# Sparse attention and two gated layers on one core: the outside keys of both heads of the first and last block are transposed together, and the sums of exponentials are finished on GpSimd

## The chip, the core and the metric

The kernel runs on one core of one Trainium2 chip. The metric is the time on the device in microseconds (us) of one execution. Five engines run side by side, each through its own instructions in order: TensorE (PE in the views, its weight loads PEld), VectorE (DVE), ScalarE (ACT), GpSimd (POOL) and the queue that issues transfers (SP).

## What is computed

Attention with a window of 32 keys to each side plus 32 global keys, for 4 batches, 8 heads, 512 local tokens and a head size of 64; its output goes through two gated layers.

```python
s_g = scale * q_g @ k_all.T                     # 32 global queries see all 544 keys
out_g = softmax(s_g) @ v_all
mask = np.abs(pos[:, None] - pos[None, :]) <= 32
s_l = np.concatenate([scale * q_l @ k_g.T, np.where(mask, scale * q_l @ k_l.T, -1e9)], -1)
out_l = softmax(s_l) @ np.concatenate([v_g, v_l])    # softmax: exp(s - max) / (sum + 1e-9)
x = heads_side_by_side(np.concatenate([out_g, out_l]))        # 2176 x 512
x = (sigmoid(x @ w_gate) * (x @ w_val)) @ w_out               # d_ff 1536
h = x @ w_in                                                  # d_ff 2048
out = (P(h) / Q(h)) @ w_out2                                  # P cubic, Q quadratic in |h|
```

## The kernel before

The kernel has three stages: attention (to about 114.6 us of the span), the first gated layer, and the rational layer. The change touches attention alone.

**Units and blocks.** Attention works on 16 units u0 to u15: a unit is one batch and one pair of heads (j = 0 and 1). A unit has four blocks c of 128 queries. An inner block (c = 1, 2) sees WIN = 224 keys: its 128 own keys, 32 global keys, and 32 keys on either side of it. An outer block (c = 0, 3) has a neighbour on one side only and sees 192 keys: 128 own and 64 outside. "Half 0" of a unit is blocks 0 and 1, "half 1" blocks 2 and 3.

**The steps of a unit**, each a small function:

- `load` (L232) issues the transfers: `kn` (keys), `qn` (queries), `vn` (values of own keys), `wn` (values of outside keys).
- `s_mm` (L256): scores of a half on TensorE into a `pair` of PSUM banks (L265). `s_max` (L270): on VectorE, scores plus mask into `p`, with the row's maximum (L277). `s_exp` (L281): on ScalarE, exponentials in place, their sum to `sum[:, n, 0]` (L285); `sum[:, n, 1]` holds 1e-9.
- `s_add` (L289) adds the two columns of `sum` into `r` (L291), `s_rec` (L293) takes the reciprocal (L295), both on VectorE; `s_norm` (L297) multiplies `p` of one block by it on GpSimd (L301).
- `t_mm` (L364): four 128x128 transposes of a block on TensorE into one PSUM bank: own keys of both heads (L368), then outside keys of both heads (L370), each padded to 128 with the last own keys. `t_out` (L374) copies the bank into `to` (L376), on ScalarE for c = 1, 3 and on VectorE for c = 0, 2.
- `v_own`, `v_edge` (L386, L395): the products with `vn` and `wn`. `wn` has zeros in its first 32 rows, and the part of `p` behind an outer block's 192 keys is zero.
- Of the global queries, per pair of units: `g_mm` (L310), `g_max`, `g_exp`, `g_rec`, `g_norm` (GpSimd, L336), `g_turn` (L342, L343), `e_own` (VectorE, L354), `e_edge` (ScalarE, L360).
- `x_hi`, `x_lo`, `x_g`, `x_out` write the result into `xh`, `xl` for the next stage (L414, L419, L427, L434, L225, L438).

**What sets the order.** The table `STEPS` gives each step a place for the first two units, a pattern of two units that repeats for the middle ones, and the last two units. All steps are sorted by place and issued in that order; each engine runs its share strictly in it. PSUM has two `pair` tiles and four `bank` tiles, handed out in the same order. The table also interleaves the preparation of the first gated weights (`w_mag`, `w_bits`, `w_add`, `w_hi`, `w_lo`).

## Time and profile before

| | |
|---|---|
| Median of 3 runs | 898.29 us (898.19 to 898.74) |
| The profiled execution: its own time | 898.83 us |
| Span in its profile | 896.9 us |
| Granted clock of TensorE | 1.00 of full speed in all 40 slices |
| Busy, share of span: PE / PEld / DVE / ACT / POOL | 99% / 82% / 84% / 64% / 64% |
| Chain of work that ended last | 87% PE, 7% DVE, 1% ACT, 1% POOL |
| Attention, first two-unit pattern to end | about 12.7 us for two units, end at 114.6 us |

Shares over the span mix stages: in attention DVE and ACT are far busier than the average says, and POOL waits for others. The stage has to be read by stretches, and then by single instructions in order of time.

### The profile page before, as it was taken

What the parts mean: (1) busy time and instruction counts of PE and PEld (TensorE: products, weight loads), DVE (VectorE), ACT (ScalarE), POOL (GpSimd) and SP (SyncE); (2) the same over time, 40 slices, a digit from 0 to 9 for tenths busy, and PEclk for the clock granted to TensorE, in tenths of its full rate; (3) what the DMA queues carried; (4) which work ended last, traced back from release to release, by engine and by line L of the source; (5) the groups of instructions that cost most, each with busy time, mean ns of one, the idle gap of its engine ahead of it and who ended that gap; (6) DMA issues with size and microseconds to landing.
All of it is one profiled execution on the core that took longest, in us unless ns stands there. A gap on an engine that the chain in (4) does not pass through costs nothing.

```text
span 896.9 us, 13592 instructions
## 1 busy us (share of the span) xinstructions
PE 889.3 (99%) x4592; PEld 737.3 (82%) x4592; DVE 750.1 (84%) x1300; ACT 576.2 (64%) x1161; POOL 576.0 (64%) x470
## 2 busy tenths in 40 slices
PE   8999999999999999999999999999999999999997
PEld 6788988888888888888888888888888888888886
DVE  6999967988889888766868699987788899888886
ACT  6999865445554344354444488777777787777773
POOL 5768765767767485476767767544555676666564
PEclk9999999999999999999999999999999999999999
DMA  9775274767667686999998960022001300110112
GB/s 307 242 219 170 83 280 169 267 227 252 232 236 262 231 300 217 322 339 321 341 352 331 360 213 1 1 94 94 1 1 51 114 24 1 43 51 1 48 59 94
DMA packets 60372, 155.87 MB, mean 174 GB/s; under 512 B 7056, under 2 KB 8720, under 8 KB 60304
## 3 DMA queue, kind: packets, MB, share of 16 engines
q1 hardware_dynamic: 60208, 154.89, 49.7%
q8 instruction: 36, 0.59, 0.3%
q14 instruction: 32, 0.26, 0.1%
q10 hardware_dynamic: 96, 0.13, 0.1%
HBM read 102.83 MB, written 52.17 MB: 173 GB/s over the span
## 4 chain that ended last, share of the span: by engine, by line
PE 87%; DVE 7%; ACT 1%; POOL 1%; issue 0%; POOLq 0%; ACTq 0%
PE rp L1255 6%; PE rp L1257 6%; PE rp L1256 6%; PE rp L725 5%; PE rp L723 5%; PE rp L724 5%; PE p L844 4%; PE p L842 4%; PE p L843 4%; PE pg L723 3%; PE pg L724 3%; PE pg L725 3%; PE pv L723 3%; PE pv L724 3%; PE pv L725 3%; PE pair L265 2%
## 5 line engine op out<-in xcount | busy, mean ns | idle before, releaser
L1172 POOL TENSOR_TENSOR v<-v,u 128x512 f32<-128x512 f32 x68 | 93.4, 1374 | 105.6 <-ACT v L1168 103.4
L1226 POOL TENSOR_TENSOR rgl<-t,rgh 128x512 fp32r<-128x512 f32 x64 | 89.1, 1393 | 40.6 <-POOL v L1172 17.3
L1255 PE MATMUL rp<-wide,rgh 128*128 128x512 f32 x204 | 79.5, 390 | 0.6 <-DVE racc L1276 0.6
L1257 PE MATMUL rp<-wide,rgl 128*128 128x512 f32 x204 | 79.4, 389 | 0.0
L1256 PE MATMUL rp<-wide,rgh 128*128 128x512 f32 x204 | 79.4, 389 | 0.0
L1165 ACT ACTIVATE u<-rp 128x512 f32<-128x512 f32 x68 | 40.5, 596 | 60.2 <-PE rp L725 57.3
L1180 DVE TENSOR_TENSOR t<-rp,t 128x512 f32<-128x512 f32 x68 | 46.7, 687 | 38.7 <-ACT t L1176 37.6
L723 PE MATMUL rp<-yh,wide 128*128 128x512 f32 x192 | 75.0, 391 | 0.0
L1205 DVE SCALAR_TENSOR_TENSOR t<-t,co,v 128x512 f32<-128x512 f32 x68 | 72.9, 1072 | 2.4
L770 ACT CAST gh<-t 128x512 fp32r<-128x512 f32 x38 | 23.6, 620 | 79.7 <-DVE t L763 76.0
L725 PE MATMUL rp<-yh,wide 128*128 128x512 f32 x192 | 74.7, 389 | 0.0
L724 PE MATMUL rp<-yl,wide 128*128 128x512 f32 x192 | 74.7, 389 | 0.0
L1201 DVE SCALAR_TENSOR_TENSOR v<-v,u 128x512 f32<-128x512 f32 x68 | 73.8, 1085 | 0.0
L301 POOL TENSOR_TENSOR p<-p,r 128x384 f32<-128x384 f32 (+1 forms) x64 | 55.4, 889 | 28.4 <-DVE r L295 13.9
L1197 DVE SCALAR_TENSOR_TENSOR v<-v,u 128x512 f32<-128x512 f32 x68 | 61.7, 908 | 1.1 <-ACT u L1193 1.1
L285 ACT ACTIVATE p<-p,mx 128x224 f32<-128x224 f32 (+1 forms) x128 | 58.5, 467 | 6.1 <-DVE mx L277 6.1
L856 DVE TENSOR_TENSOR gacc<-p,gacc 128x512 f32<-128x512 f32 x80 | 51.2, 680 | 10.1 <-PE p L844 10.1
L1168 ACT ACTIVATE v<-u,co 128x512 f32<-128x512 f32 x68 | 55.6, 817 | 2.3
L775 DVE TENSOR_TENSOR gl<-t,gh 128x512 fp32r<-128x512 f32 x38 | 37.4, 985 | 23.1 <-ACT gh L770 23.0
L1189 ACT ACTIVATE u<-v,co 128x512 f32<-128x512 f32 x68 | 49.2, 724 | 6.2 <-POOL v L1172 6.0
L1176 ACT ACTIVATE t<-rp,co 128x512 f32<-128x512 f32 x68 | 51.7, 761 | 0.0
L1214 ACT CAST rgh<-t 128x512 fp32r<-128x512 f32 x64 | 39.1, 611 | 18.0 <-DVE t L1205 18.0
(724 smaller groups left out, 2913.1 us busy)
## 6 DMA issues: line engine op xcount, KB each, us to landing
raw1gv<-in_w_gate_val SPq DMA_DIRECT2D x24, 512.0 KB, 4.2
raw2in<-in_w_in SPq DMA_DIRECT2D x16, 512.0 KB, 5.0
raw2out<-in_w_out SPq DMA_DIRECT2D x16, 512.0 KB, 5.0
kn<-in_k_l SPq DMA_DIRECT2D x15, 448.0 KB, 5.5
raw1out<-in_w_out SPq DMA_DIRECT2D x12, 512.0 KB, 4.2
vn<-in_v_l SPq DMA_DIRECT2D x16, 256.0 KB, 3.2
out<-racc SPq DMA_DIRECT2D x16, 256.0 KB, 2.0
qn<-in_q_l SPq DMA_DIRECT2D x15, 256.0 KB, 4.5
```

The costliest lines, as they stand in the source:

```text
L285: nc.scalar.activation(p, p, AF.Exp, bias=s["mx", half][:, n : n + 1], scale=-1.0, accum_out=s["sm", half][:, n, 0:1])
L723: nc.tensor.matmul(ps, wh, mh[:, k], start=k == 0, stop=False)
L724: nc.tensor.matmul(ps, wh, ml[:, k], start=False, stop=False)
L725: nc.tensor.matmul(ps, wl, mh[:, k], start=False, stop=k == 3)
L1172: nc.gpsimd.tensor_tensor(s["v"], s["v"], s["u"], ALU.mult)
L1197: nc.vector.scalar_tensor_tensor(s["v"], s["v"], Q_CONST, s["u"], ALU.add, ALU.mult)
L1201: nc.vector.scalar_tensor_tensor(s["v"], s["v"], 2.0, s["u"], ALU.subtract, ALU.mult)
L1205: nc.vector.scalar_tensor_tensor(s["t1"], s["t1"], a0, s["v"], ALU.add, ALU.mult)
L1226: nc.gpsimd.tensor_tensor(s["gl"], s["t1"], s["gh"].bitcast(F32), ALU.subtract)
L1255: nc.tensor.matmul(ps, gh[:, w], wh, start=k == 0, stop=False)
L1256: nc.tensor.matmul(ps, gh[:, w], wl, start=False, stop=False)
L1257: nc.tensor.matmul(ps, gl[:, w], wh, start=False, stop=k == G - 1)
```

## The change

The table `STEPS` is left as it is. What changes:

- **Keys on both sides.** For an outer block the 64 outside keys lie in `kn` both ahead of and behind the 128 own keys. Head 0 uses own keys then outside keys, head 1 outside keys then own keys; the two results of 192 are put side by side in `p`, so that the middle 128 of the 384 columns are the outside keys of both heads.
- **One transpose for both heads.** `t_mm` of an outer block issues three transposes, not four. `t_out` copies three of them. `v_edge` multiplies that one part by `wn`, now laid out on the host as full 128 rows with zeros in the place of the other head. The memsets of `wn` and of the end of `p` go.
- **Masks.** Masks of up to 320 columns are put together by five copies on VectorE; before it was two copies.
- **Global queries.** `g_mm` reads its 512 own keys as two pieces of 256 (six matmuls, not four). `g_norm` gets one more GpSimd copy of 128x32. `e_edge` becomes two VectorE copies of 64x32 per unit in place of one ScalarE copy of 128x64.
- **Sums.** `s_add` moves from VectorE (a reduction) to GpSimd (an addition of two columns).
- **Transfers.** `kn` grows from 448 to 480 KB a unit, `wn` from 192 to 256 KB.

```diff
-    kept = dict(kn=slots(one, "kn", 4, [128, NBLK, WIN]), ...
+    kept = dict(kn=slots(one, "kn", 4, [128, KAT[-1]]), ...
...
-    for t in wn:
-        nc.gpsimd.memset(t[0 : 128 - EDGE], 0.0)
...
-    for t in kept["p"].tiles:
-        for c in (0, NBLK - 1):
-            nc.gpsimd.memset(t[:, c, :, KEYS[c] :], 0.0)
...
     def s_add(u, half):
         r = st[u]["r", half] = two.tile([128, 4], F32, tag="r", name=f"r{u}_{half}", bufs=6)
-        nc.vector.tensor_reduce(r, st[u]["sm", half], mybir.AxisListType.X, ALU.add)
+        n = st[u]["sm", half]
+        nc.gpsimd.tensor_tensor(r, n[:, :, 0], n[:, :, 1], ALU.add)
...
-        for at, n, keys in ((0, S, lambda k: k[:, :, 0:128]), (S, SG, lambda k: k[:, 0, 128:160])):
+        for at, n, keys in ((0, 256, lambda k: own(k, 64, 0, KAT[1] - 64)), (256, 256, lambda k: own(k, 384, 96, 64 + WIN)),
+                            (S, SG, lambda k: k[:, 384 : 384 + SG])):
...
         nc.gpsimd.tensor_tensor(n, n, st[u]["gsm"].to_broadcast([128, S + SG]), ALU.mult)
+        copy(pgn[u // 2 % 2][:, S + 64 : S + 64 + SG], n[:, S:])
...
-        at = 64 * (u % 2)
-        src = st[u - u % 2]["ge"][:, at : at + 64].rearrange("p (h g) -> p h g", h=2)
-        nc.scalar.copy(turned(u)[:, 0, 2:4, 128:160], src)
+        for j in range(2):
+            rows, at = slice(64 * j, 64 * j + 64), 64 * (u % 2) + SG * j
+            nc.vector.tensor_copy(turned(u)[rows, 0, 2, 128:160], st[u - u % 2]["ge"][rows, at : at + SG])
...
-            nc.tensor.transpose(ps[:, 128 * j : 128 * j + 128], s["p"][:, c, j, 0:128], ident)
-        for j in range(2):
-            nc.tensor.transpose(ps[:, 256 + 128 * j : 384 + 128 * j], s["p"][:, c, j, EDGE:WIN], ident)
+            own = probs(u, c, j)[:, KEYS[c] - 128 :] if c in OUTER and j else probs(u, c, j)[:, 0:128]
+            nc.tensor.transpose(ps[:, 128 * j : 128 * j + 128], own, ident)
+        if c in OUTER:
+            nc.tensor.transpose(ps[:, 256:384], s["p"][:, c].rearrange("p j k -> p (j k)")[:, 128:256], ident)
+        else:
+            for j in range(2):
+                nc.tensor.transpose(ps[:, 256 + 128 * j : 384 + 128 * j], s["p"][:, c, j, EDGE:WIN], ident)
...
-        (nc.scalar.copy if c in T_ACT else nc.vector.tensor_copy)(turned(u)[:, c, :, at : at + 128], src)
+        (nc.scalar.copy if c in T_ACT else nc.vector.tensor_copy)(turned(u)[:, c, 0:n, at : at + 128], src)
...
-                             turned(u)[:, c, 2 + j, SG * (c % 2) : SG * (c % 2) + n],
+                             turned(u)[:, c, 2 + (0 if c in OUTER else j), SG * (c % 2) : SG * (c % 2) + n],
```

**Where `s_add` lands in the queues, at the start.** GpSimd's order for unit u0. `p_111` is u0's `p`, `pgn_125` the global queries' `p`; `r_1_...` belongs to half 1 and `r_0_...` to half 0. Before:

```order
L301 TENSOR_TENSOR p_111<-p_111,r_1_227 128x448 [waits DVE_49,Activation_49]
L336 TENSOR_TENSOR pgn_125<-pgn_125,gsm_218 128x544 [waits DVE_49,Activation_49]
L301 TENSOR_TENSOR p_111<-p_111,r_0_260 128x2x192 [waits DVE_49]
L301 TENSOR_TENSOR p_111<-p_111,r_0_260 128x448 [waits Activation_49]
L301 TENSOR_TENSOR p_111<-p_111,r_1_227 128x2x192
```

Now:

```order
L314 TENSOR_TENSOR p_111<-p_111,r_1_223 128x448 [waits DVE_49]
L351 TENSOR_TENSOR pgn_125<-pgn_125,gsm_214 128x544 [waits DVE_49,Activation_49]
L231 TENSOR_TENSOR pgn_125<-pgn_125,zero 128x32 [waits Pool_49]
L301 TENSOR_TENSOR r_0_257<-sum_132 128x4 [waits Activation_49]
L314 TENSOR_TENSOR p_111<-p_111,r_0_257 128x384 [waits DVE_49]
L314 TENSOR_TENSOR p_111<-p_111,r_0_257 128x448
L314 TENSOR_TENSOR p_111<-p_111,r_1_223 128x384
```

The sum of half 0 now stands behind the global queries' normalization and its new copy on GpSimd.

**The same at the end.** GpSimd's order for the last units. `p_112` is u13's, `p_113` u14's, `p_111` u15's; L434, L225 and L438 are `x_out`. Before:

```order
L301 TENSOR_TENSOR p_112<-p_112,r_1_1464 128x2x192 [waits DVE_49,PE_49,Activation_49]
L301 TENSOR_TENSOR p_112<-p_112,r_1_1464 128x448
L301 TENSOR_TENSOR p_113<-p_113,r_0_1502 128x2x192 [waits DVE_49,PE_49,Activation_49]
L301 TENSOR_TENSOR p_113<-p_113,r_0_1502 128x448
L336 TENSOR_TENSOR pgn_126<-pgn_126,gsm_1403 128x544 [waits DVE_49]
L301 TENSOR_TENSOR p_113<-p_113,r_1_1493 128x2x192 [waits Activation_49]
L301 TENSOR_TENSOR p_113<-p_113,r_1_1493 128x448 [waits PE_49]
L434 TENSOR_TENSOR xga_169<-xga_169 128x4x32 [waits DVE_49]
```

Now (twelve rows, in which the sums of u14's half 1 and half 0 and of u15's half 0 and half 1 stand between the normalizations):

```order
L301 TENSOR_TENSOR r_1_1498<-sum_137 128x4 [waits Activation_49]
L314 TENSOR_TENSOR p_112<-p_112,r_1_1469 128x384 [waits DVE_49,PE_49]
L314 TENSOR_TENSOR p_112<-p_112,r_1_1469 128x448
L301 TENSOR_TENSOR r_0_1507<-sum_136 128x4
L314 TENSOR_TENSOR p_113<-p_113,r_0_1507 128x384 [waits DVE_49,PE_49]
L314 TENSOR_TENSOR p_113<-p_113,r_0_1507 128x448
L351 TENSOR_TENSOR pgn_126<-pgn_126,gsm_1408 128x544 [waits DVE_49]
L231 TENSOR_TENSOR pgn_126<-pgn_126,zero 128x32 [waits Pool_49]
L301 TENSOR_TENSOR r_0_1580<-sum_132 128x4 [waits Activation_49]
L314 TENSOR_TENSOR p_113<-p_113,r_1_1498 128x384
L301 TENSOR_TENSOR r_1_1603<-sum_133 128x4 [waits Activation_49]
L314 TENSOR_TENSOR p_113<-p_113,r_1_1498 128x448 [waits PE_49]
```

Two normalizations of u13 now come after a sum that needs u14's exponentials, and u14's last one after a sum that needs u15's.

VectorE's order at the same place, before:

```order
L291 TENSOR_REDUCE r_1_1493<-sum_140 128x4 [waits Activation_49]
L295 RECIPROCAL r_1_1493<-r_1_1493 128x4 [waits DVE_49]
L291 TENSOR_REDUCE r_0_1502<-sum_139 128x4
L295 RECIPROCAL r_0_1502<-r_0_1502 128x4 [waits DVE_49]
L427 COPY xga_169<-bank_96 128x32 [waits PE_49]
L331 TENSOR_SCALAR gsm_1403<-gsm_1403 128x1
```

Now:

```order
L305 RECIPROCAL r_1_1498<-r_1_1498 128x4 [waits Pool_49]
L305 RECIPROCAL r_0_1507<-r_0_1507 128x4 [waits Pool_49]
L448 COPY xga_163<-bank_96 128x32 [waits PE_49,Activation_49]
L346 TENSOR_SCALAR gsm_1408<-gsm_1408 128x1
L347 RECIPROCAL gsm_1408<-gsm_1408 128x1 [waits DVE_49]
```

The two reductions are gone, and both reciprocals wait for GpSimd.

## Rows read from the trace of the kernel before

**Rows 1.** Busy time by stretch: us, PE, PEld, DVE, ACT, POOL, clock, DMA share, GB/s.

```profile
25.00:30.00 5.00, 5.00 (x45) 3.29 (x43) 4.93 (x34) 5.00 (x23) 2.65 (x3) 1.00 0.99 314
50.00:100.00 50.00, 50.00 (x560) 44.28 (x556) 46.60 (x237) 46.88 (x177) 35.62 (x43) 1.00 0.58 177
250.00:300.00 50.00, 50.00 (x224) 41.34 (x223) 44.58 (x58) 25.28 (x48) 32.13 (x24) 1.00 0.68 235
```

**Rows 2.** TensorE in order of time: start us, us, engine, line, tiles [idle before].

```profile
76.41 1.11 PE L310 MATMUL pair<-kn,qgn 128*64 128x512 f32 x8
77.46 0.44 PE L368 MATMUL bank<-ident,p 128*128 128x128 f32 x2
...
79.91 1.68 PE L265 MATMUL pair<-kn,qn 64*128 64x192 f32 x16
...
92.59 1.68 PE L265 MATMUL pair<-kn,qn 64*128 64x192 f32 x16
...
94.69 0.38 PE L368 MATMUL bank<-ident,p 128*128 128x128 f32 x2
...
95.13 0.38 PE L368 MATMUL bank<-ident,p 128*128 128x128 f32 x2
...
110.40 0.49 PE L386 MATMUL bank<-to,vn 128*64 128x160 f32 x4
```

**Rows 3.** Idle time inside the two-unit pattern: VectorE and GpSimd in order of time.

```profile
88.52 0.19 DVE L427 COPY xga<-bank 128x32 f32<-128x32 f32 x1 [1.14 <-ACT xh L414]
...
81.96 1.72 POOL L301 TENSOR_TENSOR p<-p,r 128x384 f32<-128x384 f32 x2 [1.86 <-DVE r L295]
```

**Rows 4.** Groups by line and shape, 0 to 135 us: count | busy us, mean ns.

```profile
L301 POOL TENSOR_TENSOR p<-p,r 128x448 f32<-128x448 f32 x32 | 30.5, 952 | 10.7 <-DVE r L295 10.5 <-DVE xga L427 0.2
L301 POOL TENSOR_TENSOR p<-p,r 128x384 f32<-128x384 f32 x32 | 26.5, 827 | 17.7 <-ACT p L285 12.1 <-DVE r L295 3.4 <-PE pair L265 0.8
...
L376 DVE COPY to<-bank 128x512 f32<-128x512 f32 x32 | 21.0, 678 | 0.6 <-PE bank L370 0.6
...
L427 DVE COPY xga<-bank 128x32 f32<-128x32 f32 x32 | 5.6, 182 | 6.0 <-ACT xh L414 5.5 <-PE bank L395 0.4
...
L360 ACT COPY to<-bank 128x64 f32<-128x64 f32 x16 | 2.5, 217 | 0.0
...
L208 POOL MEMSET sum<- 128x8 f32 x6 | 0.3, 94 | 0.0
```

**Rows 5.** The start: GpSimd and VectorE in order of time.

```profile
12.47 1.09 POOL L336 TENSOR_TENSOR pgn<-pgn,gsm 128x544 f32<-128x544 f32 x1
14.03 2.50 POOL L301 TENSOR_TENSOR p<-p,r 128x384 f32<-128x384 f32 x3 [0.46 <-DVE r L295]
...
13.58 0.16 DVE L291 TENSOR_REDUCE r<-sum 128x4 f32<-128x8 f32 x1
13.77 0.18 DVE L295 RECIPROCAL r<-r 128x4 f32<-128x4 f32 x1
```

**Rows 6.** The end: ScalarE, VectorE and GpSimd in order of time.

```profile
99.03 0.20 ACT L285 ACTIVATION_READ_ACCUMULATOR p<-p,mx 128x1 f32 x1
...
105.51 0.19 ACT L285 ACTIVATION_READ_ACCUMULATOR p<-p,mx 128x1 f32 x1
...
99.72 0.18 DVE L295 RECIPROCAL r<-r 128x4 f32<-128x4 f32 x1
...
100.57 0.19 DVE L427 COPY xga<-bank 128x32 f32<-128x32 f32 x1 [0.33 <-ACT xh L414]
...
103.38 0.08 DVE L277 DVE_READ_ACCUMULATOR2_ANT mx<- 128x1 f32 x1
...
104.48 0.46 POOL L434 TENSOR_TENSOR xga<-xga 128x128 f32<-128x128 f32 x1
...
106.12 1.72 POOL L301 TENSOR_TENSOR p<-p,r 128x448 f32<-128x448 f32 x2 [0.18 <-DVE xga L427]
108.00 1.72 POOL L301 TENSOR_TENSOR p<-p,r 128x384 f32<-128x384 f32 x2 [0.16 <-DVE r L295]
```

More of the change, by code (lines that the diff above doesn't have):

```diff
@@ L189, in attention, with mask_of, probs @@
     st = [dict() for _ in units]
-    masks = one.tile([128, 2, WIN], F32, name="masks")
-    m = masks[:, 1]
-    mask_of = [masks[:, 0]] + [m] * (NBLK - 1)
+    masks = one.tile([128, 3, 320], F32, name="masks")
+    m = masks[:, 1, 0:WIN]
+    def mask_of(c, j):
+        if c in OUTER:
+            return masks[:, 2 if c else 0, 128 * j : 128 * j + KEYS[c]]
+        return m
+    def probs(u, c, j):
+        if c in OUTER:
+            return st[u]["p"][:, c].rearrange("p j k -> p (j k)")[:, j * KEYS[c] : (j + 1) * KEYS[c]]
+        return st[u]["p"][:, c, j]
     still = one.tile([128, 128], F32, name="still")
@@ L199, in attention @@
     nc.vector.memset(m, 0.0)
-    pgn = [one.tile([128, S + EDGE], F32, name=f"pgn{i}") for i in range(2)]
+    pgn = [one.tile([128, S + 128], F32, name=f"pgn{i}") for i in range(2)]
     wn = [one.tile([128, NBLK, 128], F32, name=f"wn{i}") for i in range(3)]
@@ L264, in s_mm @@
                 rows = slice(64 * j, 64 * j + 64)
-                nc.tensor.matmul(ps[:, j, i * WIN : i * WIN + KEYS[c]], s["qn"][rows, c], s["kn"][rows, c, 0 : KEYS[c]],
+                at, to = KAT[c] + (64 if c in OUTER and j == 0 else 0), i * WIN
+                nc.tensor.matmul(ps[:, j, to : to + KEYS[c]], s["qn"][rows, c], s["kn"][rows, at : at + KEYS[c]],
                                  start=True, stop=True)
@@ L297, in s_norm @@
     def s_norm(u, half, i):
-        n = KEYS[2 * half + i]
-        p = st[u]["p"][:, 2 * half + i, :, 0:n]
+        c = 2 * half + i
+        n = KEYS[c]
+        p = st[u]["p"][:, c]
+        if c in OUTER:
+            p = p.rearrange("p j k -> p (j k)")[:, 0 : 2 * n].rearrange("p (j k) -> p j k", j=2)
         r = st[u]["r", half][:, 2 * i : 2 * i + 2].unsqueeze(2).to_broadcast([128, 2, n])
@@ L1369, in laid @@
     own, edge = pairs(x["k_l"], x.pop("k_g"))
-    x["k_l"] = np.concatenate([own, edge], axis=1).transpose(2, 3, 4, 0, 1)
+    out = [edge[c, 0:64] for c in OUTER]
+    k = [out[0], own[0], out[0], own[1], edge[1], own[2], edge[2], out[1], own[3], out[1]]
+    x["k_l"] = np.concatenate(k).transpose(1, 2, 3, 0)
     own, edge = pairs(x["v_l"], x.pop("v_g"))
-    x["v_l"], x["w_l"] = own.transpose(2, 3, 1, 0, 4), edge.transpose(2, 3, 1, 0, 4)
+    w = np.zeros((NBLK, 128) + edge.shape[2:], edge.dtype)
+    for c in range(NBLK):
+        if c in OUTER:
+            for j in range(2):
+                w[c, 64 * j : 64 * j + 64, ..., 64 * j : 64 * j + 64] = edge[c, 0:64, ..., 64 * j : 64 * j + 64]
+        else:
+            w[c, 128 - EDGE :] = edge[c]
+    x["v_l"], x["w_l"] = own.transpose(2, 3, 1, 0, 4), w.transpose(2, 3, 1, 0, 4)
     q = x["q_g"].reshape(B, 2, 2, 2, SG, D)
```

23 lines of the change are left out of this document (15 added, 8 removed).

## The prediction

> **What bounds the kernel now.** I read the busy time by stretch first. TensorE is busy for all 50 us of 50 to 100 and of 250 to 300 [rows 1]: both in attention and in the gated layers the end is set by TensorE, at full clock. So a microsecond by which attention's matmuls end earlier or later is, to a first reading, a microsecond of the kernel: behind attention nothing is changed. But inside attention the reader should see how little room there is: from 50 to 100 us VectorE is busy 46.6 and ScalarE 46.9 of 50, and from 25 to 30 us, while the units start up, ScalarE is busy without a gap and VectorE 4.93 of 5 [rows 1]. There it is these two that set the pace.
>
> Second, TensorE in order of time. The same row of scores returns at 79.91 and 92.59 [rows 2]: two units take 12.68 us. In that pattern the other engines have some room: VectorE stands still for 1.14 us before 88.52, GpSimd for 1.86 us before 81.96 [rows 3]. Third, the end of attention, engine by engine [rows 6]: there the pattern breaks off, GpSimd works through its last normalizations until 109.7 (108.00 + 1.72), and TensorE's last transposes end at 110.40 [rows 2], just behind it.
>
> **What is removed from TensorE.** Two transposes in each unit, 32 in all. From 94.69 to 95.13 four transposes are issued [rows 2], 0.11 us each: 3.5 us. It counts only where TensorE sets the pace. That is not so for u0 to u2 (before about 33 us), nor, as shown below, for the end (u11 to u15). Between lie u3 to u10: 16 transposes, **-1.8 us**.
>
> **What is added to TensorE.** `g_mm` issues 12 records where it issued 8; the columns are the same. The eight take 1.05 us (76.41 to 77.46 [rows 2]). If the loads of weights stay hidden behind 256 columns, this costs nothing; I take that, since 0.11 us transposes hide a load of 128 columns each. If each extra record costs as much as an eighth of the row, it is 32 x 0.13 = 4 us; I hold a quarter of that for an upper bound, 1 us.
>
> **ScalarE and VectorE in the pattern.** ScalarE loses `e_edge` (0.217 us, 16 times) and a quarter of one 128x512 copy per unit. VectorE loses a reduction per half (0.16 us [rows 5]) and a quarter of a 0.678 us copy per unit, and gains two small copies per unit, each at most the 0.182 us of the 128x32 copy [rows 4]. Per two units that is -0.6 - 0.3 + 0.7, about zero; the 1.14 us of idle covers the error. If it were gone, VectorE would become the bound (a rival below).
>
> **GpSimd: prices.** No row shows a 128x4 addition there. The nearest below is the 128x8 memset, 0.094 us [rows 4]; the nearest above the 128x128 addition, 0.46 us [rows 6]. Between 384 and 448 columns a row grows by 0.125 us (827 to 952 ns [rows 4]), 2 ns a column; taken off the 0.46 us this leaves 0.2 us for `s_add` and 0.3 us for the new 128x32 copy, which I use. [...]
>
> The price is small. What costs is the place: `s_add` waits for ScalarE's exponentials at the head of GpSimd's queue, with other units' normalizations behind it, and VectorE's reciprocal now waits for GpSimd, with scores behind it. Inside the pattern I went through the four sums of two units: GpSimd waits for the exponentials a few tenths, the 1.86 us of idle absorbs it, and TensorE's transposes read normalized blocks 2 us and more after they are done. Cost there: zero. The two ends differ.
>
> **The start.** In u0, GpSimd's normalization of the global queries ends at 13.56 (12.47 + 1.09) and half 0's reciprocal is issued at 13.77 [rows 5]. Now the sum stands behind that normalization and its copy: 13.56 + 0.3 + 0.2, 0.1 for the handover (13.95 to 14.03 [rows 5]) and 0.1 for larger key transfers at a DMA share of 0.99 [rows 1] make 14.26: 0.5 us late. VectorE's first four `e_edge` copies (up to 0.7 us), less a reduction and a quarter of a copy (0.3 us), bring it to some 0.7 us. VectorE and ScalarE carry that without a gap to 30 us, winning back about 0.3 us in reductions and shorter copies on the way. TensorE arrives at 33 us **0.4 us later** (bounds: -0.2, where the saved memsets and reductions win; +0.9).
>
> **The end.** All times here are on the clock of the trace, as if nothing had shifted before. u14's half 1 has its exponentials at 99.23 (99.03 + 0.20 [rows 6]); with ScalarE's savings, 98.9. Only then GpSimd's sum runs, and behind it u13's two normalizations and the sum of half 0: 98.9 + 0.2 + 1.7 + 0.2 = 101.0. VectorE's reciprocal of half 0, at 99.72 before [rows 6], waits until 101.1: 1.4 us late. Of that, the 0.33 us it stood idle before 100.57 is free. So the maxima of u15's half 1, done at 103.38 + 0.08 before, are done at about 104.5, and the exponentials of that half, done at 105.70 (105.51 + 0.19), at 106.2 (between 105.7, if ScalarE catches all up, and 106.8, if nothing). GpSimd's last sum waits for these at the head of its queue. Before, u14's last normalization and `x_out` were done by then: `x_out` starts at 104.48 and u15's normalizations at 106.12 [rows 6]. Now both lie behind the sum: 106.2 + 0.2, 0.95 for the normalization, 1.46 for `x_out` (104.48 to 106.12 less the 0.18 wait), 3.44 for u15's four normalizations (106.12 to 109.72 less the 0.16 wait): 112.25. TensorE's last block needs the last of them and takes 0.44 us: 112.7, where the rows have 110.40. **+2.3 us** (bounds +1.4 and +2.8); the transposes saved in u11 to u15 vanish in this wait.
>
> **The sum.** -1.8 + 0.4 + 2.3 = +0.9 us. The profiled execution took 898.83 us, 1.9 us more than its span, so 899.7; the median of the runs, 898.29, lies 0.5 us lower, and I predict against it: 899.2 us. The bounds of the terms (-1.8 to -0.8, -0.2 to +0.9, +1.4 to +2.8) allow this case 897.7 to 901.2. A measurement of this kernel can tell about 0.2%, 1.8 us, from no change, so that its middle is "the same".
>
> **Rivals.**
> 1. *The ends do not bind.* If GpSimd's and VectorE's late sums are absorbed at the end as in the pattern, all transposes after the start count: -3.5 + 0.4 = -3.1, 895.2 us. For it: GpSimd works 36 of 50 us from 50 to 100 [rows 1], and its waits are mostly for others. Against it: before the change the last normalization and the last transposes already follow each other within 0.7 us. Chance 0.20.
> 2. *Slower: small GpSimd operations cost what a 128x128 addition costs.* At 0.46 us for each sum and copy, the start loses 0.4 us more and the three sums in the chain of the end 0.8 us; in the pattern GpSimd then has 7.1 us of normalizations, 1.1 of the global queries, some 1.3 of weights and 2.3 of small operations for 12.3 us, so that its waits reach VectorE, some 0.3 us per pattern, 1.2 us. Together 2.4 us more: 901.6 us. It is slower by more than 0.2% from about 0.33 us per operation on. Chance 0.12.
> 3. *VectorE becomes the bound of the pattern*, because the reciprocals wait and the small copies come on top: the 1.8 us are not won, and 0.4 + 2.3 = +2.7 remain, 901.0 us. For it: 93% busy; against it: the 1.14 us of idle. Chance 0.10.
>
> **How the numbers follow.** The forecast has 0.58, of which about 0.08 lies over 900.1. Faster: rival 1, 0.20. Slower: 0.12 + 0.10 + 0.08 = 0.30. The same: 0.50. The range reaches from 895.3, which cuts rival 1 about in half, to 901.6, which cuts rival 2 in half; outside lie under 0.2.
>
> **What would show it.** In the profile after: the distance between the returning rows of scores falls by 0.4 us (else rival 3). At the start GpSimd's first sum of half 0 begins only after the copy, and VectorE shows a wait for GpSimd ahead of that reciprocal. Near the end VectorE stands still for over 1 us for GpSimd ahead of u14's second reciprocal, and TensorE's last transposes wait for GpSimd, with the first products behind them about 2 us later than 12.3 us patterns would give. The 128x4 addition's own row says whether rival 2 lives. If TensorE shows no wait for GpSimd in the last 12 us of attention, the prediction is wrong and rival 1 right.

## The result: 0.6% slower, all of it lost in attention

| | before | after |
|---|---|---|
| Median of 6 runs each | 898.76 us | 904.31 us |
| Ratio to before | | 1.0060, 95% interval 1.0047 to 1.0072 |
| Profiled execution: span | 896.9 us | 902.0 us |
| First matmul of the gated layers | 114.58 us | 120.03 us |
| Row of 16 score matmuls that opens the first full pattern | 29.77 us | 30.14 us |
| From there over five patterns to the last such row | 62.82 us | 64.32 us |
| From that row to the first gated matmul | 21.99 us | 25.57 us |

The forecast was 899.2 us with a range up to 901.6; the kernel lies outside it. The median is 5.55 us longer, and the first gated matmul already comes 5.45 us later. The last three lines of the table split the loss: +0.4 us at the start, +1.5 us over five patterns of two units where the prediction had a gain, +3.6 us at the end where it had +2.3.

The kernel after, busy time by stretch, columns as in [rows 1]:

```profile
50.00:100.00 50.00, 48.31 (x538) 42.16 (x536) 46.29 (x231) 43.57 (x161) 37.45 (x60) 1.00 0.59 190
250.00:300.00 50.00, 50.00 (x224) 41.37 (x223) 45.07 (x55) 24.39 (x45) 36.80 (x26) 1.00 0.74 253
```

TensorE had no gap from 50 to 100 us before [rows 1]; now 1.7 us are missing there, though it has less to do. In these 50 us ScalarE is busy 3.3 us less, VectorE only 0.3.

TensorE of the kernel after in order of time: two returning rows of scores, the waits for VectorE behind them, and the waits at the end.

```profile
81.57 1.68 PE L274 MATMUL pair<-kn,qn 64*128 64x192 f32 x16
...
86.18 0.97 PE L274 MATMUL pair<-kn,qn 64*128 64x224 f32 x8 [0.20 <-DVE mx L286]
87.09 0.49 PE L407 MATMUL bank<-to,vn 128*64 128x160 f32 x4
...
94.46 1.68 PE L274 MATMUL pair<-kn,qn 64*128 64x192 f32 x16
...
98.39 0.97 PE L274 MATMUL pair<-kn,qn 64*128 64x192 f32 x8 [0.57 <-DVE mx L286]
...
106.75 0.66 PE L358 MATMUL bank<-ident,pgn 128*128 128x128 f32 x4 [0.73 <-POOL pgn L351]
...
112.17 0.44 PE L385 MATMUL bank<-ident,p 128*128 128x128 f32 x2 [0.52 <-POOL p L314]
...
113.92 0.44 PE L385 MATMUL bank<-ident,p 128*128 128x128 f32 x2 [0.66 <-POOL p L314]
...
115.26 0.44 PE L385 MATMUL bank<-ident,p 128*128 128x128 f32 x2 [0.47 <-POOL p L314]
...
115.85 0.49 PE L407 MATMUL bank<-to,vn 128*64 128x160 f32 x4
...
120.03 0.50 PE L744 MATMUL pg<-xh,wide 128*128 128x512 f32 x1
```

From 81.57 to 94.46 are 12.89 us (the three patterns ahead of it take 12.91 to 13.31); before it was 12.68 [rows 2]. Inside a pattern TensorE now waits for VectorE's maxima: the scores of the second half need a `pair` tile that these maxima still read. At the end it waits for GpSimd's normalizations, and the first product of the last units starts at 115.85, where it was 110.40 [rows 2].

Two different engines, two places. VectorE in the stretch between the two rows of scores, the kernel before:

```profile
81.02 0.15 DVE L291 TENSOR_REDUCE r<-sum 128x4 f32<-128x8 f32 x1
81.09 0.35 DVE L277 CUSTOM_DVE_ANT_0 p<-pair,masks 128x192 f32<-128x192 f32 x1
...
81.64 0.17 DVE L295 RECIPROCAL r<-r 128x4 f32<-128x4 f32 x1
81.73 0.36 DVE L277 CUSTOM_DVE_ANT_0 p<-pair,masks 128x224 f32<-128x224 f32 x1
```

and the kernel after, with the edge copies (L376) in the same places:

```profile
82.64 0.38 DVE L376 COPY to<-bank 64x32 f32<-64x32 f32 x2
83.05 0.36 DVE L286 CUSTOM_DVE_ANT_0 p<-pair,masks 128x192 f32<-128x192 f32 x1
...
83.61 0.39 DVE L376 COPY to<-bank 64x32 f32<-64x32 f32 x2
84.03 0.18 DVE L305 RECIPROCAL r<-r 128x4 f32<-128x4 f32 x1
84.24 0.39 DVE L286 CUSTOM_DVE_ANT_0 p<-pair,masks 128x224 f32<-128x224 f32 x1
```

What counts in a queue without gaps is the time from one start to the next. The reduction that is gone had 0.15 us but took the queue only 0.07 (81.02 to 81.09). Two edge copies take 0.41 and 0.42, and the reciprocal behind the second pair takes 0.21, where it took 0.09 (81.64 to 81.73). Two bank copies ahead of them, one of which is now shorter, take 0.14 less (81.58 to 82.64; before 79.82 to 81.02). That is 0.41 + 0.42 + 0.12 - 0.07 - 0.14 = +0.74 us in this pattern, in the one stretch of VectorE's queue for which TensorE waits.

TensorE shows how much of it arrives. The first product behind the second half's scores came 5.11 us after the first row of scores before (79.91 [rows 2] to 85.02):

```profile
85.02 0.49 PE L386 MATMUL bank<-to,vn 128*64 128x160 f32 x4
```

Now it comes 5.52 us after (81.57 to 87.09), 0.41 later, although two transposes (0.22 us) fewer stand ahead of it. The rest of the pattern is 0.20 us shorter, and +0.21 is left.

The single edge copies of one pair, and the bank copy ahead of them, show where the time goes:

```profile
82.04 0.68 DVE L397 COPY to<-bank 128x512 f32<-128x512 f32 x1
82.64 0.17 DVE L376 COPY to<-bank 64x32 f32<-64x32 f32 x1
82.82 0.19 DVE L376 COPY to<-bank 64x32 f32<-64x32 f32 x1
```

The first copy (rows 0 to 63) begins 0.08 us before the bank copy ahead of it has ended (82.72). The second (rows 64 to 127) begins only when the first has ended (82.81), and the maximum behind the pair, of all rows again, only at 83.05, after the second has ended (83.02). The other edge copies of this kernel do the same (last section). So it is not that a copy has 64 rows: the first has 64 too and is not late. What is late is the instruction that begins at another row than the one ahead of it. Behind the second pair it is the reciprocal, and then also the maximum, the first to read PSUM again after the copies.

The end of the kernel after, GpSimd and then VectorE:

```profile
101.55 0.20 POOL L301 TENSOR_TENSOR r<-sum 128x4 f32<-128x4 f32 x1 [0.93 <-ACT p L294]
101.70 1.72 POOL L314 TENSOR_TENSOR p<-p,r 128x384 f32<-128x384 f32 x2
103.38 0.20 POOL L301 TENSOR_TENSOR r<-sum 128x4 f32<-128x4 f32 x1
...
108.72 0.20 POOL L301 TENSOR_TENSOR r<-sum 128x4 f32<-128x4 f32 x1 [0.78 <-ACT p L294]
...
111.19 4.02 POOL L314 TENSOR_TENSOR p<-p,r 128x448 f32<-128x448 f32 x4
```

```profile
101.78 0.18 DVE L305 RECIPROCAL r<-r 128x4 f32<-128x4 f32 x1 [0.59 <-POOL r L301]
103.61 0.18 DVE L305 RECIPROCAL r<-r 128x4 f32<-128x4 f32 x1 [1.65 <-POOL r L301]
```

This is the chain that the prediction described: the sum of u14's half 1 waits for its exponentials at the head of GpSimd's queue, u13's two normalizations (1.7 us) follow, then the sum of half 0, and VectorE's reciprocal of half 0 stands still for it 1.65 us. The sum itself is cheap, as its group (count | busy us, mean ns | idle before) shows, and so is the new copy:

```profile
L301 POOL TENSOR_TENSOR r<-sum 128x4 f32<-128x4 f32 x32 | 7.2, 227 | 13.1 <-ACT p L294 12.9
...
L231 POOL TENSOR_TENSOR pgn<-pgn,zero 128x32 f32<-128x32 f32 x8 | 1.9, 238 | 0.6
```

### The profile page after: what moved, and what is told of

The parts are those of the page before. It is cut to its first block, busy times and chain, and to the rows that moved or that the text cites. A ratio compares the mean times of both kernels' runs of the same rounds, so it can differ in the third digit from the quotient of the medians.

```text
span 902.0 us, 13608 instructions
## 1 busy us (share of the span) xinstructions
PE 887.2 (98%) x4592; PEld 734.9 (81%) x4592; DVE 753.3 (84%) x1303; ACT 574.2 (64%) x1145; POOL 581.7 (64%) x501
## 4 chain that ended last, share of the span: by engine, by line
PE 84%; DVE 10%; POOL 2%; ACT 1%; issue 1%; DMA 1%; SPq 0%; POOLq 0%; ACTq 0%
PE rp L1276 6%; PE rp L1278 6%; PE rp L1277 6%; PE rp L744 5%; PE rp L746 5%; PE rp L745 5%; PE p L865 4%; PE p L863 4%; PE p L864 4%; PE pg L744 3%; PE pg L746 3%; PE pg L745 3%; PE pv L744 3%; PE pv L746 3%; PE pv L745 3%; PE pair L274 1%
```

## The experiments

All runs are read by the same three stretches of TensorE's order of time: the start of the row of 16 score matmuls near 30 us (A), from it over five patterns to the last such row (B), and from there to the first gated matmul (C). Each kernel has one profile. A lies anywhere between 29.3 and 31.0 us, for causes that were not separated.

| Kernel | A | B | C | first gated | median us | ratio to before, 95% interval |
|---|---|---|---|---|---|---|
| before | 29.77 | 62.82 | 21.99 | 114.58 | 898.76 | |
| after | 30.14 | 64.32 | 25.57 | 120.03 | 904.31 | 1.0060 (1.0047, 1.0072) |
| e1_sum_back | 30.42 | 65.59 | 22.98 | 118.99 | 903.00 | 1.0041 (1.0029, 1.0054) |
| e2_edge_back | 30.50 | 62.47 | 25.82 | 118.79 | 902.63 | 1.0036 (1.0023, 1.0049) |
| e3_both_back | 29.73 | 62.82 | 22.65 | 115.20 | 900.59 | 1.0013 (1.0004, 1.0022) |
| e4_before_sum | 30.56 | 62.64 | 25.20 | 118.40 | 902.68 | 1.0034 (1.0020, 1.0047) |
| e5_before_edge | 30.51 | 63.41 | 22.06 | 115.98 | 900.03 | 1.0003 (0.9994, 1.0011) |
| e6_before_split | 29.94 | 63.69 | 22.00 | 115.63 | 899.84 | 1.0003 (0.9994, 1.0011) |
| e7_sum_split | 30.07 | 62.10 | 22.67 | 114.84 | 898.86 | 0.9991 (0.9982, 0.9999) |
| e8_no_sum | 30.00 | 62.28 | 22.26 | 114.54 | 898.19 | 0.9993 (0.9985, 1.0002) |
| e9_before_edge64 | 29.89 | 67.50 | 23.18 | 120.57 | 905.70 | 1.0067 (1.0055, 1.0079) |
| e10_edge128 | 30.64 | 61.98 | 25.14 | 117.76 | 901.58 | 1.0025 (1.0017, 1.0034) |
| e11_turn32 | 29.51 | 62.99 | 22.08 | 114.58 | 898.82 | 0.9994 (0.9985, 1.0002) |
| e12_turn_no_sum | 29.87 | 63.43 | 22.08 | 115.38 | 898.72 | 0.9990 (0.9982, 0.9999) |
| e13_loads | 29.32 | 62.07 | 22.08 | 113.47 | 898.61 | 0.9991 (0.9982, 1.0000) |
| e14_before_loads | 29.91 | 62.74 | 21.98 | 114.63 | 899.25 | 1.0003 (0.9994, 1.0011) |
| e15_no_sum_loads | 30.97 | 62.21 | 22.08 | 115.26 | 898.33 | 0.9987 (0.9978, 0.9996) |

Ratios of the experiments are to runs of before side by side with them, whose medians lay between 899.2 and 899.4 us.

### Two parts undone, one at a time, and one done alone

**e1_sum_back:** after, sums on VectorE.

```diff
-        nc.gpsimd.tensor_tensor(r, n[:, :, 0], n[:, :, 1], ALU.add)
+        nc.vector.tensor_reduce(r, n, mybir.AxisListType.X, ALU.add)
```

> The changed kernel with the sums of exponentials back on VectorE; all else as changed. Read from the two traces, the changed kernel loses 0.4 us up to the row of scores at 30.14 us, 1.5 us over the five patterns from there to the row at 94.46, and 3.6 us from that row to the first gated matmul at 120.03. Theory (two causes in two places: the sums in GpSimd's queue cost the end, the edge copies on VectorE cost the pattern): the stretch from the last row of 16 score matmuls to the first gated matmul falls from 25.6 to about 21.5 us, the pattern stays at 13.0 us or over, since VectorE gets its reductions back and keeps the copies: 900 to 901.5 us. Rival A (all of the loss is VectorE's work in the pattern; GpSimd's sums are harmless): the reductions come on top, 904.5 to 906 us. Rival B (all of the loss is GpSimd's sums): 896 to 898 us.

C falls by 2.6 us, and B grows by 1.3: the end is GpSimd's, the pattern is not, and VectorE's reductions come on top of a queue that already sets the pattern. Neither rival fits. The time, 903.0, lies above the theory's 900 to 901.5: the growth of B had been left out, and C stops 1.5 us above the 21.5 us that it gave.

**e2_edge_back:** after, edge copies on ScalarE, still of 64 rows.

```diff
-            nc.vector.tensor_copy(turned(u)[rows, 0, 2, 128:160], ...
+            nc.scalar.copy(turned(u)[rows, 0, 2, 128:160], ...
```

> The changed kernel with the edge copies back on ScalarE, as two copies of 64 rows; the sums stay on GpSimd. Theory (two causes): the pattern falls from 13.0 us to between 12.3 and 12.7, the wait of the second half's scores for VectorE's maxima goes, the end keeps its 25 us: 901 to 902.8 us. Rival A (VectorE's work is all): 895 to 897 us. Rival B (GpSimd's sums are all): 904 us, unchanged, with the pattern still at 13 us.

As the theory has it: B falls by 1.9 us (with one wait of 0.9 us for a transfer in it), C stays. VectorE waits for GpSimd at the end as in the kernel after, at the same two reciprocals:

```profile
100.54 0.18 DVE L305 RECIPROCAL r<-r 128x4 f32<-128x4 f32 x1 [1.61 <-POOL r L301]
102.37 0.18 DVE L305 RECIPROCAL r<-r 128x4 f32<-128x4 f32 x1 [1.65 <-POOL r L301]
```

**e3_both_back:** both edits above; the shared transposes and the layout remain.

> The shared transposes and the new layout of keys alone: sums on VectorE, edge copies on ScalarE. Theory (two causes): both losses go, and TensorE keeps the saved transposes where it sets the pace: pattern 12.3 us, 895.5 to 897 us, that is 1.8 to 3.3 us under the kernel before. Rival C (layout, larger transfers, the split global scores or the new copy on GpSimd cost something of their own): 898.5 us or more, with a pattern of 12.7 us or a later start.

The theory missed here, and rival C came out. B is 62.82 us, that of before, though each pattern has 0.44 us fewer transposes, and C is 0.7 us longer. That B agrees to the hundredth is chance: its five patterns take 12.3 to 13.0 us, where the last four of before all take 12.7. So the shared transposes by themselves gain nothing in this form, and the layout costs something at the end.

**e4_before_sum:** the kernel before, with the sums on GpSimd.

```diff
-        nc.vector.tensor_reduce(r, st[u]["sm", half], mybir.AxisListType.X, ALU.add)
+        n = st[u]["sm", half]
+        nc.gpsimd.tensor_tensor(r, n[:, :, 0], n[:, :, 1], ALU.add)
```

> The kernel before with the sums of exponentials moved to GpSimd alone. Theory (two causes): the pattern stays at 12.7 us, the start loses up to 0.3 us, the end loses the 2.3 us that the prediction put there or more, up to the 3.6 us of the changed kernel: 901 to 902.5 us; VectorE shows a wait of over 1 us for GpSimd ahead of u14's reciprocals, TensorE waits for GpSimd's normalizations ahead of its last transposes. Rival A: within 1 us of before, or faster by the reductions that VectorE loses. Rival B: 904 us.

B stays, C grows by 3.2 us. Moving the sums costs 2.6 to 3.2 us at the end, whatever else is changed (after against e1, e2 against e3, e4 against before). In the pattern it costs nothing; where VectorE sets the pattern, it saves (after against e1).

### What the edge copies cost

**e5_before_edge:** the kernel before, edge copies on VectorE, cut by columns.

```diff
-        nc.scalar.copy(turned(u)[:, 0, 2:4, 128:160], src)
+        for j in range(2):
+            nc.vector.tensor_copy(turned(u)[:, 0, 2 + j, 128:160], src[:, j])
```

> The kernel before with its edge copies on VectorE, two copies per unit of 128x32 each; nothing else. Theory (VectorE has no room in the stretch between two rows of scores, whatever its idle time elsewhere): four copies of 0.2 us land there, the pattern grows from 12.7 to 13.1 us or more, five patterns +2 to +2.8 us, the end stays at 22 to 22.5 us: 901 to 902.5 us. Rival (the prediction's step: the idle of 1.1 us in each pattern covers the copies): pattern 12.7 us, 899.4 us as before.

The theory that any four copies break VectorE's stretch fell: B grows by 0.6 us (one late pattern of 13.3 us, the others 12.0 to 12.7), and the time cannot be told from before. As many copies, on the same engine, at the same places, are nearly free here and cost 1.9 to 2.8 us of B in the changed kernel. What differs is the form of the copies, and the layout around them. VectorE of this kernel:

```profile
56.32 0.28 DVE L361 COPY to<-bank 128x32 f32<-128x32 f32 x2
56.52 0.15 DVE L291 TENSOR_REDUCE r<-sum 128x4 f32<-128x8 f32 x1
...
57.14 0.28 DVE L361 COPY to<-bank 128x32 f32<-128x32 f32 x2
57.34 0.17 DVE L295 RECIPROCAL r<-r 128x4 f32<-128x4 f32 x1
57.42 0.36 DVE L277 CUSTOM_DVE_ANT_0 p<-pair,masks 128x224 f32<-128x224 f32 x1
```

Two copies of all 128 rows take the queue 0.20 us, half of what two copies of 64 rows took, although a single one has the same duration (181 and 183 ns); and the reciprocal behind them takes 0.08 and not 0.21.

**e9_before_edge64:** the kernel before, the same copies cut by rows.

```diff
-        nc.scalar.copy(turned(u)[:, 0, 2:4, 128:160], src)
+        for j in range(2):
+            rows = slice(64 * j, 64 * j + 64)
+            nc.vector.tensor_copy(turned(u)[rows, 0, 2:4, 128:160], src[rows])
```

> The kernel before with its edge copies on VectorE, two copies per unit again, but cut by rows: 64 rows x 64 columns each, where the run with 128x32 copies cut by columns. With 128x32 copies the pattern stayed at 12.7 us, in the changed kernel's form (64x32) on VectorE it is 13.0 us. Theory (copies of 64 rows do not overlap with their neighbours in VectorE's queue: two of them take 0.40 us from start to next, two of 128x32 take 0.20, and the instruction behind them starts its successor 0.1 us late): the stretch between two rows of scores grows by 0.5 us beside the 128x32 run, the pattern goes to between 12.9 and 13.2 us, TensorE waits for VectorE's maxima, first gated matmul 1 us or more later than with 128x32 copies; 900.5 to 902 us. Rival (the number of copies counts, not their rows; the changed kernel's loss comes with its other layout): pattern 12.7 us, 900 us.

```profile
57.37 0.44 DVE L362 COPY to<-bank 64x64 f32<-64x64 f32 x2
57.83 0.16 DVE L291 TENSOR_REDUCE r<-sum 128x4 f32<-128x8 f32 x1
58.02 0.36 DVE L277 CUSTOM_DVE_ANT_0 p<-pair,masks 128x192 f32<-128x192 f32 x1
...
58.58 0.45 DVE L362 COPY to<-bank 64x64 f32<-64x64 f32 x2
59.07 0.18 DVE L295 RECIPROCAL r<-r 128x4 f32<-128x4 f32 x1
59.28 0.39 DVE L277 CUSTOM_DVE_ANT_0 p<-pair,masks 128x224 f32<-128x224 f32 x1
```

The rows decide: cut by rows, the same copies make the kernel before slower than the changed kernel is, 905.7 us, with 13.5 us a pattern. The direction was expected, the size not. Here the reduction behind the first pair is late as well, 0.19 us to the next start (57.83 to 58.02) where it took 0.07: two pairs, the reduction and the reciprocal make 0.46 + 0.49 + 0.12 + 0.12 = about +1.2 us in this stretch, more than the +0.74 of the changed kernel, and no reduction is gone in return. The end, C, is 1.2 us longer too; for that no cause was separated.

**e10_edge128:** after, its edge copies over all rows (the odd heads then take the even heads' probabilities for the outside keys of the global queries).

```diff
-            rows, at = slice(64 * j, 64 * j + 64), 64 * (u % 2) + SG * j
-            nc.vector.tensor_copy(turned(u)[rows, 0, 2, 128:160], st[u - u % 2]["ge"][rows, at : at + SG])
+            at = 64 * (u % 2) + SG * j
+            nc.vector.tensor_copy(turned(u)[:, 0, 2 + j, 128:160], st[u - u % 2]["ge"][:, at : at + SG])
```

> The changed kernel with its two edge copies per unit taken over all 128 rows instead of 64, the second into the part behind the first; so the odd heads' global queries miss their own outside keys in the first block, which leaves nothing out in time. Theory (64-row copies do not overlap): four of them take 0.40 us less of VectorE's stretch and the instructions behind them 0.2 us less, pattern from 13.0 to 12.4 to 12.6 us, end at 25.6 us as in the changed kernel: first gated matmul near 117.5 to 118, 901.5 to 902.5 us. Rival (the copies' rows do not matter): 904.3 us, pattern 13.0 us.

B falls from 64.32 to 61.98 us, less than before has, with the copies still on VectorE. So the whole loss in the pattern is the copies' cut by rows. C keeps its 25 us, as it should with the sums on GpSimd. This run and the kernel after differ only in the rows, and in the part that the second copy fills; e5 and e9 differ in the copies' width as well.

### The split global scores

**e6_before_split:** the kernel before, own keys of the global scores in two pieces of 256.

```diff
-        for at, n, keys in ((0, S, lambda k: k[:, :, 0:128]), ...
+        for at, n, keys in ((0, 256, lambda k: k[:, 0:2, 0:128]), (256, 256, lambda k: k[:, 2:4, 0:128]), ...
```

> The kernel before with the global scores issued as two pieces of 256 columns where it issues one of 512. Theory: no cost; start of the global scores to the start of the next transposes stays at 1.05 us, pattern 12.7 us, time as before within 0.5 us. Rival (each record costs an eighth of the row): 0.5 us per pair of units, 1 us to 4 us in all.

No cost: the twelve take 1.06 us (64.74 to 65.80 us), the eight took 1.05 [rows 2], the time is that of before. Of B's 0.9 us more, 0.7 is one wait of TensorE, at 39 us, for a transfer of the global queries; the other four patterns take 12.7 us.

### Where the saved transposes went

**e7_sum_split:** the edge copies on ScalarE, the sums on GpSimd only where no end is near.

```diff
+        if u in (0, 1, 14, 15):
+            nc.vector.tensor_reduce(r, n, mybir.AxisListType.X, ALU.add)
+        else:
             nc.gpsimd.tensor_tensor(r, n[:, :, 0], n[:, :, 1], ALU.add)
```

> Shared transposes and new layout, edge copies on ScalarE, sums on GpSimd for u2 to u13 and on VectorE for u0, u1, u14 and u15. Theory (the sums on GpSimd cost only at the start and the end, and free VectorE in the pattern, which with all sums on VectorE holds it at 12.56 us on the mean): start near 29.7 us, pattern 12.3 us, from the last row of 16 score matmuls to the first gated matmul 22.7 us: first gated matmul near 114, 0.5 to 1.3 us earlier than with all sums on VectorE, 898.5 to 900 us beside 899.4 of before. Rival (the pattern does not shorten below TensorE's former 12.56 us because another wait ends it): first gated matmul at 115.2 as with the sums on VectorE; or the end keeps over 24 us because of the sums of u12 and u13.

C is 22.67 us, where e2 with all sums on GpSimd has 25.82: the 3.2 us of the end belong to the four sums of the last two units, and the 24 sums of u2 to u13 cost nothing there. B falls to 62.10. It is the first version under before, by 0.1%.

**e8_no_sum:** the sums taken from both engines.

```diff
-        nc.gpsimd.tensor_tensor(r, n[:, :, 0], n[:, :, 1], ALU.add)
...
-        nc.vector.reciprocal(r, r)
+        nc.vector.reciprocal(r, st[u]["sm", half][:, :, 0])
```

> Shared transposes and new layout, edge copies on ScalarE, and no sums at all: the addition of 1e-9 to the sums of exponentials of the local queries is left out (each sum holds exp(0) = 1 of its own maximum, to which 1e-9 adds nothing in this type), the reciprocal reads the accumulated column itself. It takes the step away from both engines. Theory: start 29.7 us or earlier, pattern 12.3 us, end 22 to 22.5 us: first gated matmul at 113 to 114, 897.5 to 899 us, under the kernel before by 0.5 to 2 us. Rival (the saved transposes are worth nothing because the loop through ScalarE and the score tiles binds, not VectorE's load): pattern 12.6 us, first gated matmul at 115, 900 us.

62.28 us in B: even with the step gone from both engines, four fewer transposes give 0.1 us a pattern and not 0.44. C, 22.26 us, is still longer than before's. The first gated matmul, 114.54 us, misses the theory's 113 to 114.

**e11_turn32:** as e7, and the turn of the outside keys made so that one copy of 128x32 per unit does.

```diff
-        copy(pgn[u // 2 % 2][:, S + 64 : S + 64 + SG], n[:, S:])
...
-        nc.tensor.transpose(st[u]["ge"][:, 0:128], g[:, S : S + 128], ident)
+        for j in range(2):
+            of = ident.rearrange("p (u h g) -> p u h g", u=2, h=2)[:, :, j]
+            nc.tensor.matmul(st[u]["ge"][64 * j : 64 * j + 64, 0:64], g[:, S : S + 64], of, start=True, stop=True)
...
-        for j in range(2):
-            rows, at = slice(64 * j, 64 * j + 64), 64 * (u % 2) + SG * j
-            nc.scalar.copy(turned(u)[rows, 0, 2, 128:160], st[u - u % 2]["ge"][rows, at : at + SG])
+        at = SG * (u % 2)
+        nc.scalar.copy(turned(u)[:, 0, 2, 128:160], st[u - u % 2]["ge"][:, at : at + SG])
```

> Shared transposes and new layout; sums on GpSimd for u2 to u13, on VectorE for u0, u1, u14 and u15; and the outside keys of the global queries turned by two products with chosen columns of the identity, one for each head's rows, so that the new copy on GpSimd goes and one ScalarE copy of 128x32 per unit stands where two of 64x32 stood. Theory (the 0.7 us that the end still loses beside the kernel before are ScalarE's 0.4 us for four 64-row copies and GpSimd's 0.24 us copy in its chain): from the last row of 16 score matmuls to the first gated matmul 22.0 us, where the run with the sums split has 22.7; pattern 12.4 us; first gated matmul at 113.5 to 114.3, 897.5 to 898.7 us. Rival (the end is set elsewhere): 22.7 us, 898.9 us as with the sums split.

C is 22.08 us, as expected: ScalarE's four copies of 64 rows and GpSimd's copy, together, were what the layout cost at the end. ScalarE of the kernel before and of e3, the same place:

```profile
92.54 0.34 ACT L360 COPY to<-bank 128x64 f32<-128x64 f32 x2
92.73 0.52 ACT L285 ACTIVATE p<-p,mx 128x224 f32<-128x224 f32 x1
```

```profile
92.51 0.77 ACT L376 COPY to<-bank 64x32 f32<-64x32 f32 x4
93.30 0.48 ACT L294 ACTIVATE p<-p,mx 128x224 f32<-128x224 f32 x1
```

Two copies of 128 rows take 0.19 us, four of 64 rows 0.79. But B is not shorter than before's, because of one wait, TensorE of e11:

```profile
76.31 1.17 PE L328 MATMUL pair<-kn,qgn 128*64 128x256 f32 x12 [1.04 <-DMA qgn<-in_q_g]
```

**e12_turn_no_sum:** e11 without sums.

> The same as the run with products by chosen columns of the identity, and no sums at all: the addition of 1e-9 to the sums of the local queries' exponentials is left out, the reciprocal reads the accumulated column itself. Theory: nothing stands in GpSimd's or VectorE's queue for the sums; pattern 12.3 us, end 21.7 to 22 us, first gated matmul at 113 to 114, 896.8 to 898.2 us, 0.15% or more under the kernel before. Rival (the loop through ScalarE and the two score tiles holds the pattern at 12.6 us whatever is taken from VectorE): 898.5 us or more.

The same C, 22.08 us, and the same wait for that transfer (1.14 us, up to 77.12). With it the first gated matmul comes at 115.38 us, and the theory's 113 to 114 is missed.

**e13_loads, e14_before_loads, e15_no_sum_loads:** e11, before and e12 with two transfers moved.

```diff
-    ('load', 'w', (-28.52292, 6.10594, 6.86833, 6.60856, 7.04185, 5.77992)),
-    ('g_load', (-193.6, None, 4.1758, None, -6.26303, None)),
+    ('load', 'w', (-28.52292, 6.10594, 6.86833, 7.2, 7.04185, 5.77992)),
+    ('g_load', (-193.6, None, 3.9, None, -6.26303, None)),
```

> The run with products by chosen columns of the identity and sums split between the engines, with two transfers moved in the queue that issues them: the global queries' ahead of the keys of the same pair of units, and the outside values' (256 KB) behind these keys. In that run TensorE waited 1.0 us, once, at 76.3 us, for the global queries' transfer, which stood behind 1.5 MB of others. Theory (the pattern that the shared transposes shorten now meets the transfers, and this wait is what hides the gain): the wait goes, the row of scores after it comes 1 us sooner, first gated matmul 113.4 to 113.8 (114.58 there), 897.3 to 898.2 us. Rival (the transfers are late in any order, or ScalarE and VectorE are late anyway): another wait of 0.5 us or more takes its place, 898.8 us as there.

> The kernel before with the same two transfers moved; nothing else. It tells apart what the moved transfers give by themselves. Theory: TensorE did not wait for a transfer at 76 us in the kernel before, so nothing changes, 899.3 us, pattern 12.7 us. Rival: the order of transfers is worth 0.5 us or more by itself.

> The run with products by chosen columns of the identity and no sums (the addition of 1e-9 left out), with the same two transfers moved. There TensorE waited 1.1 us for the global queries' transfer at 77.1 us. Theory: the wait goes, first gated matmul 113.5 to 114.3 (115.38 there), 897 to 898 us, 0.15% or more under the kernel before. Rival: 898.7 us as there.

In e13 the wait is gone, and the first gated matmul comes at 113.47 us, 1.1 us before those of e11 and of the kernel before; nothing changes in the control. Beside e11, 0.9 us of it lie in B and 0.2 in A. So for this profile the theory holds. The profiled execution, 897.17 us, is also the fastest of the eleven. The medians tell less: 898.61 against e11's 898.82 is within what they can tell apart. In e15 the wait for the transfer is gone too, and B falls from 63.43 to 62.21 us; but at 28.4 us, ahead of A, TensorE waits 0.9 us for VectorE's reciprocals, so that the first gated matmul (115.26) stays outside the theory's 113.5 to 114.3. Its ratio is the lowest of all, 0.9987. The versions whose interval lies under 1, e7, e12 and e15, are faster than before by about 0.1%, which is little for a choice among fifteen runs; of these, only e7 adds the 1e-9 as the reference writes it.

## Why the prediction was wrong, step by step

**ScalarE and VectorE in the pattern: the step that failed.** The prediction set -0.6 - 0.3 + 0.7 against each other and got about zero; the stretch shows +0.74. Two errors, both of one kind: it added durations of single instructions, and in a queue without gaps they overlap. The reductions were credited at 0.16 us each and were worth 0.07. The edge copies were charged 0.18 us each from the 128x32 copy of [rows 4], which is the right duration, but the row is of copies of 128 rows, which take the queue 0.10 (e5, 56.32 to 56.52 for two); cut by rows they take 0.20 from start to next, and hold up what follows by 0.12. The Trainium skill has the rule (VectorE: DVE Perf Modes, section "Two Vector instructions with no wait between them"): an instruction whose input or output starts in another group of 32 partitions than the last one in that memory starts only when all earlier ones have finished. The runs agree: e5 and e9 copy the same data and differ only in how it is cut, the kernel after and e10 differ in the rows of the copies, and the reciprocal (its output) and the maximum behind it (its input from PSUM) are both late, as the rule says. So is the second copy of a pair and not the first. The prediction looked up what each moved operation costs, and not what it does to its neighbours.

**"The 1.14 us of idle covers the error."** It does not, for it lies elsewhere. VectorE's idle [rows 3] comes while it waits for ScalarE ahead of `x_g`, after the maxima; from there to the last maximum of the next row of scores its queue has no gap. With copies of 128 rows four patterns of five kept their length all the same (e5), with copies of 64 rows none did. So rival 3, VectorE becoming the bound, is what happened, with the copies, and not reciprocals that wait, as the cause: its chance of 0.10 was too small, and its price, only the loss of the 1.8 us, too low. The pattern went past its old length.

**The transposes, -1.8 us.** 0.11 us each is right: from a row of 16 score matmuls to that of the second half TensorE needs 3.29 us with the shared transposes (e13, 53.39 to 56.68 us) and 3.50 before, 0.21 less for two. But the pattern was not TensorE's alone: with sums and edge copies on their former engines (e3) nothing is won, with the sums out of its way (e7) 0.14 us a pattern, with the step gone (e8) 0.11, not 0.44. TensorE without a gap in [rows 1] did not say how soon the next engine would be in the way. The other way round, the prediction left out u0 to u2 because VectorE and ScalarE were to set the pace there, although its own row has TensorE busy for 5.00 of 5 us from 25 to 30 us as well; in e13 it is the first pattern that is shortened most, 11.52 us (29.32 to 40.84) against 12.08 before (29.77 to 41.85).

**The end, +2.3 us.** The mechanism is the one described, and both signs named for it are in the trace: a stand of 1.65 us ahead of u14's second reciprocal, and TensorE's waits for normalizations. The size was too small. The sums alone cost 2.6 to 3.2 us (three pairs of runs), over the upper bound of 2.8 in two of them; the rest of the 3.6 is the layout's. The kernel after can be laid beside the prediction's chain by taking off the 1.87 us by which its last row of scores is later (94.46 against 92.59). ScalarE was taken to be 0.3 us early with u14's exponentials, with GpSimd's sum at 98.9; it starts at 99.7 (101.55), and the last sum at 106.85 (108.72) in place of 106.2: +0.65. From there to u15's normalizations the chain took 2.46 us, not 2.61: -0.15. These four took 4.02 us (111.19 to 115.21), not 3.44: +0.58. The first product came 0.64 us behind them, not 0.44: +0.20. Together they are the 1.3 us that were missing. Why u14's exponentials are late was not separated: with the edge copies on ScalarE (e2) four copies take it 0.79 us where two took 0.19, and in the kernel after VectorE's maxima are late (TensorE's 0.57 us wait at 98.39). The last two normalizations of u15 took 1.01 and 1.38 us, where the same two shapes took 0.83 and 0.93 before; they run beside an instruction of VectorE on two operands that prepares the gated weights, as in the last section:

```profile
113.22 1.20 DVE L607 SCALAR_TENSOR_TENSOR v11gv<-raw1gv,v11gv 128x512 uint32<-128x512 uint32 x1
113.83 1.38 POOL L314 TENSOR_TENSOR p<-p,r 128x448 f32<-128x448 f32 x1
```

**The start, +0.4 us.** Measured +0.37, within the scatter of A. The path was the one described in part: the sum stands behind the copy, and VectorE waits for it (0.24 us),

```profile
12.84 0.24 POOL L231 TENSOR_TENSOR pgn<-pgn,zero 128x32 f32<-128x32 f32 x1
13.04 0.20 POOL L301 TENSOR_TENSOR r<-sum 128x4 f32<-128x4 f32 x1
```

but the normalization ahead of them began 0.8 us earlier than before (11.67 us; 12.47 in [rows 5]), so that the reciprocal came at 13.27 and not at 14.3. A does not settle the term: kernels with the first sums on GpSimd have it at 30.1 to 30.6 us, those without at 29.3 to 30.1, but e1, e5 and e15, without them too, at 30.4 to 31.0.

**GpSimd's prices and the split scores were right.** A sum has a median of 198 ns (0.2 assumed), the copy 238 ns (0.3 assumed), so rival 2 is out. Two of the 32 sums took 0.64 us (last section). "Cost there: zero" holds for the sums in the pattern (e4: B 62.64 against 62.82). The split costs nothing (e6).

**Rival 1, ends that do not bind,** had 0.20 and is out; TensorE's waits for GpSimd in the last 12 us were the test that the prediction set for it.

Put together: -1.8 should have been about +1.5 (copies of 64 rows on VectorE, in the one stretch without slack), 2.3 should have been 3.6, and 0.4 was measured, though not shown to come from the sums: +5.5 us.

**Not settled.** With sums and copies out of the way B divided by five is 12.4 to 12.6 us, where TensorE's saving alone would give 12.1 (12.56 - 0.44). In e13 three of the last four patterns take 12.55 or 12.56 us, those of before 12.68; there the transposes of the global queries, with the two products that turn the outside keys, take 0.26 us more than before (77.13 to 77.93 against 78.39 to 78.93), so that 12.50 were to be expected, which leaves little open. For e7 and e8 the traces show small waits, for maxima, exponentials and transfers in turn, and no single cause was separated.

## What to carry to other kernels

Price an instruction that moves to a busy queue by the time from its start to the next start, its neighbours' included, and look at which rows it and its neighbours begin: split a small copy by columns, not by rows. An engine's idle time counts only in the stretch in which somebody waits for it. A step that moved to another engine's in-order queue was harmless in the steady pattern here and expensive where the pattern ends; try such a move without the last units.
